# Weight loads that cast on their way, and two-kilobyte q and k loads, in a fused sliding-window attention and MLP kernel

## The chip, the cores and the metric

The kernel runs on one core of one Trainium2 chip. The metric is the device time of one execution in microseconds (us). The profile lists busy time of a tensor engine (PE), VectorE (DVE), ScalarE (ACT) and GpSimd (POOL), and none of SyncE (SP), which issues transfers: 105 in after. ScalarE and GpSimd issue transfers too, between their other instructions (5 and 8 in after). The profile gives the time of the transfers as a share of 16 DMA engines.

## The reference

Attention with a window of 128 tokens and four "sink" tokens that every later token may see, then a two-layer MLP with a quick GELU:

```python
# q, k, v: (4 batches, 8 heads, 768 tokens, 64), float32
scores = (1 / sqrt(64)) * q @ k.T
keep   = (pos_k < 4) | ((0 <= pos_q - pos_k) & (pos_q - pos_k < 128))
a      = softmax(where(keep, scores, -1e9))
x      = (a @ v) as (3072 tokens, 512)
h      = x @ w_in                        # w_in (512, 2048) float32
g      = h / (1 + exp(-1.702 * h))
out    = g @ w_out                       # w_out (2048, 512) float32
```

## The kernel before

The tokens are worked on in 12 blocks of 256. Block k needs its q, k and v (512 KB each in float32), their cast to float16, the transposes of q and k, the scores and the rest of the attention; after it the first layer, which needs `w_in`, and later the second, which needs `w_out`. The two weights are 8 chunks of 1 MB, four of each. Blocks 0 to 2 and the weights have to come in during the first 40 us or so, while the tensor engine is already working on what has arrived.

The order of the instructions on each engine is fixed by a planner that runs when the program is built. It keeps a clock of its own for each engine and one for the transfers, picks the next instruction by priority, and sorts the program by the planned start.

```python
class Plan:
    def run(self, ...):
        dma_free = 0.0                        # ONE clock for all transfers
        ...
            s = max([free[e]] + [after(d, e) for d in o.deps])
            if isinstance(o.engs[e][1], tuple) and len(landed) >= LANES:   # LANES = 8
                s = max(s, landed[-LANES])
        ...
                begin = max(s + 1300, dma_free)       # a transfer begins when those
                dma_free = begin + ns                 # planned before it have ended
                ...
        order.sort(key=lambda x: (x[0], x[1]))        # the program is this ORDER only
```

In the program an instruction waits for data that it reads and for a buffer that it overwrites (one of SyncE's loads of v waited 4.1 us for a cast of v). If it issues a transfer it waits at times for an earlier one that it neither reads nor overwrites: SyncE's loads of q and k waited 1.1 us, in two waits, for v to land. The planner counts this as lanes, eight of them: it issues a transfer when the eighth before it has landed.

The weights are loaded as float32 into a ring of three buffers by SyncE, and cast in halves, 15 of the 16 by GpSimd and one by ScalarE:

```python
    CAST_W = ["POOL ACT"] + ["POOL"] * 7
    def weights(j, at):
        dst = w32[j % RW]                             # RW = 3
        war = reuse("w32", j % RW)
        src = ... 1 MB of moe_w_in (j < 4) or moe_w_out ...
        o_l = op("SP", 400, (2880, 32), lambda: nc.sync.dma_start(dst, src), war, prio=at, kind="w")
        loads.append(o_l)
        for n in range(2):
            to, fr = ...                              # half a chunk
            o = plan.any(cast(1024, CAST_W[j]), lambda e, to=to, fr=fr: copy(e, to, fr), [o_l], ...)

    LOADS = ["a0", "a1", "w0", "w1", "w2", "w3", "a2", "w4", "w5", "w6", "w7"]   # a0: block 0
```

q and k are loaded with two tokens to a partition, which makes runs of 512 bytes in memory; for blocks 0 to 2 (`KT = 3`) they are transposed on the tensor engine, one pair of heads at a time, each pair as soon as its part is there:

```python
        if k == 0:      # three pieces each: q by SyncE, k by ScalarE
            for n, (p0, p1) in enumerate(((0, 1), (1, 2), (2, 4))):
                ...
        else:
            nc.sync.dma_start(dst[:, e], src[b, :, t0 : t0 + TB].rearrange("h (p i) d -> p h i d", i=2))
    ...
        def tp():       # in front(k, p): one pair of heads
            for i in range(2):
                for e in range(2):
                    nc.tensor.transpose(ps[:, e, :, i, :],
                        c16[:, i, e, 2 * p : 2 * p + 2].rearrange("s h d -> s (h d)"), ident)
```

In the first 14 us the tensor engine fills its gaps with matmuls on zeros (line 788 in before), which count as busy (10.2 us in before) and do no work.

The softmax here doesn't subtract the row's maximum and nothing guards it: scores larger than these inputs give would overflow.

## Time and profile before

| | before |
|---|---|
| time, median of 3 | 228.54 us (228.28 to 228.6) |
| span of the profiled execution | 225.9 us |
| tensor engine busy | 216.6 us (96 %) |
| idle time of the tensor engine, 225.9 - 216.6 | 9.3 us |
| tensor engine's share of the chain of waits | 88 % |
| first first-layer matmul | 20.75 us |

From the page of before, the span, the busy times, and two rows of the 40 slices (5.65 us each): the busy share of the DMA engines in tenths and what they moved, in GB/s. Bytes are counted as they are written, which will matter later (in after, the queue with the casting transfers shows 4.19 MB for the 8.39 MB of float32 that they read):

```profile
span 225.9 us, 5365 instructions
PE 216.6 (96%) x2122; PEld 150.2 (66%) x2122; DVE 127.5 (56%) x278; ACT 130.7 (58%) x259; POOL 104.0 (46%) x177
...
DMA  6999999999499999899696895892902402410232
GB/s 169 287 326 375 337 347 352 337 282 239 100 251 288 226 197 220 215 181 288 113 226 176 169 254 121 157 269 61 187 1 49 93 3 46 93 41 8 46 69 70
...
PE 88%; ACT 4%; DVE 3%; DMA 2%; issue 1%; ACTq 0%
```

The last line is the chain of waits. The tensor engine bounds the kernel, so only time in which it is idle or fills gaps can be won. The table by stage of before shows where that is; its columns are the window, its length, busy time (and instructions) of each engine, the granted clock of the tensor engine, the DMA share (the time that packets took, over 16 engines; it comes out above 1 at times and serves here only to tell busy from idle), and GB/s:

```profile
0.00:20.00 20.00, 17.59 (x259) 13.97 (x260) 12.14 (x41) 12.11 (x26) 13.09 (x29) 1.00 0.95 280
20.00:40.00 20.00, 19.39 (x229) 15.59 (x226) 17.10 (x39) 15.07 (x31) 14.89 (x18) 1.00 1.07 347
40.00:60.00 20.00, 20.00 (x159) 13.46 (x157) 8.34 (x17) 7.37 (x13) 17.13 (x27) 1.00 1.06 261
60.00:80.00 20.00, 18.24 (x197) 11.58 (x196) 12.39 (x29) 12.49 (x28) 15.16 (x27) 1.00 1.06 230
```

Apart from the start, the tensor engine loses 0.6 us between 20 and 40 us and 1.8 us between 60 and 80 us, and 4.6 us after 80 us, at the very end. The DMA engines are busy at 90 % and more from 6 to 56 us.

How the weights come in, from the timeline of GpSimd in before (start, length, instruction; in brackets the idle time before it and what ended it):

```profile
18.16 1.04 POOL L274 CAST w_in<-w 128x1024 f16<-128x1024 f32 x1 [0.19 <-DMA w<-in_moe_w_in_dram]
...
20.81 2.03 POOL L274 CAST w_in<-w 128x1024 f16<-128x1024 f32 x2 [1.61 <-DMA w<-in_moe_w_in_dram]
23.57 2.03 POOL L274 CAST w_in<-w 128x1024 f16<-128x1024 f32 x2 [0.73 <-DMA w<-in_moe_w_in_dram]
26.27 2.03 POOL L274 CAST w_in<-w 128x1024 f16<-128x1024 f32 x2 [0.67 <-DMA w<-in_moe_w_in_dram]
```

Each of the last three casts waited for its chunk, so the chunks landed 2.7 us apart. No other load was put among them, as the timeline of SyncE in before shows: the four chunks of `w_in` go out in a row, and block 2's q is issued only after them:

```profile
9.97 10.66 SPq L331 DMA_DIRECT2D w<-in_moe_w_in_dram  x4
20.68 1.35 SPq L385 DMA_DIRECT2D qk<-in_q_dram  x1
...
26.23 3.35 SPq L331 DMA_DIRECT2D w<-in_moe_w_out_dram  x3
```

### The profile page before, as it was taken

What the parts mean: (1) busy time and instruction counts of PE and PEld (TensorE: products, weight loads), DVE (VectorE), ACT (ScalarE), POOL (GpSimd) and SP (SyncE); (2) the same over time, 40 slices, a digit from 0 to 9 for tenths busy, and PEclk for the clock granted to TensorE, in tenths of its full rate; (3) what the DMA queues carried; (4) which work ended last, traced back from release to release, by engine and by line L of the source; (5) the groups of instructions that cost most, each with busy time, mean ns of one, the idle gap of its engine ahead of it and who ended that gap; (6) DMA issues with size and microseconds to landing.
All of it is one profiled execution on the core that took longest, in us unless ns stands there. A gap on an engine that the chain in (4) does not pass through costs nothing.

```text
span 225.9 us, 5365 instructions
## 1 busy us (share of the span) xinstructions
PE 216.6 (96%) x2122; PEld 150.2 (66%) x2122; DVE 127.5 (56%) x278; ACT 130.7 (58%) x259; POOL 104.0 (46%) x177
## 2 busy tenths in 40 slices
PE   8989999999988999999999999999999999999991
PEld 8766886666644776767667667666667667666640
DVE  2677989533376574965565555556457456433400
ACT  3659579154378369746747747645856846445310
POOL 6486777789939981756609729119200000000000
PEclk9999999999999999999999999999999999999999
DMA  6999999999499999899696895892902402410232
GB/s 169 287 326 375 337 347 352 337 282 239 100 251 288 226 197 220 215 181 288 113 226 176 169 254 121 157 269 61 187 1 49 93 3 46 93 41 8 46 69 70
DMA packets 73976, 41.07 MB, mean 182 GB/s; under 512 B 29792, under 2 KB 66784, under 8 KB 73952
## 3 DMA queue, kind: packets, MB, share of 16 engines
q1 hardware_dynamic: 72128, 39.72, 71.2%
q10 hardware_dynamic: 1824, 1.02, 1.6%
q8 instruction: 16, 0.26, 0.5%
q14 instruction: 8, 0.07, 0.1%
HBM read 27.36 MB, written 6.29 MB: 149 GB/s over the span
## 4 chain that ended last, share of the span: by engine, by line
PE 88%; ACT 4%; DVE 3%; DMA 2%; issue 1%; ACTq 0%
PE bank L694 36%; PE bank L722 36%; PE bank L627 6%; PE bank L572 4%; ACT at L590 3%; DMA qk<-in_k_dram 2%; DVE at L597 2%; PE bank L788 2%; PE bank L537 1%; PE bank L511 1%; PE bank L666 1%; ACT ats L545 0%; DVE xn L647 0%; DVE qkT L520 0%; DVE gT L708 0%
## 5 line engine op out<-in xcount | busy, mean ns | idle before, releaser
L722 PE MATMUL bank<-w_out,gT 128*128 128x512 f16 x384 | 99.1, 379 | 0.0
L694 PE MATMUL bank<-xT,w_in 128*128 128x256 f16 x768 | 98.8, 273 | 0.1
L706 ACT ACTIVATE th<-bank 128x512 f16<-128x512 f32 x96 | 57.6, 603 | 62.4 <-PE bank L694 61.5
L708 DVE SCALAR_TENSOR_TENSOR gT<-th,bank 128x512 f16<-128x512 f16 x96 | 65.4, 684 | 49.2 <-ACT th L706 49.1
L694 PEld LDWEIGHTS <-w_in 128*128 128x128 f16 x768 | 73.3, 98 | 21.6 <-issue 2.0
L274 POOL CAST qk<-qk 64x512 f16<-64x512 f32 (+1 forms) x78 | 47.5, 612 | 38.2 <-DMA qk<-in_q_dram 34.4
L590 ACT ACTIVATE at<-bank 128x512 f16<-128x512 f32 (+1 forms) x96 | 50.0, 575 | 5.4 <-PE bank L572 5.0
L722 PEld LDWEIGHTS <-gT 128*128 128x128 f16 x384 | 35.7, 98 | 24.4 <-issue 0.8
L597 DVE TENSOR_TENSOR at<-at,bank 128x1024 f16<-128x1024 f16 (+1 forms) x48 | 30.5, 637 | 20.9 <-ACT at L590 20.8
L274 POOL CAST v<-v 64x512 f16<-64x512 f32 (+1 forms) x48 | 28.6, 595 | 5.0 <-DMA v<-in_v_dram 2.7
L627 PE MATMUL bank<-v,at 128*128 128x65 f16 x352 | 21.4, 193 | 2.0 <-DVE at L597 1.9
L627 PEld LDWEIGHTS <-at 128*128 128x128 f16 x352 | 17.2, 97 | 7.6 <-DVE at L597 3.8
L740 ACT ACTIVATE osb<-bank 128x512 f32<-128x512 f32 (+1 forms) x24 | 14.2, 592 | 11.0 <-PE bank L722 10.9
L545 ACT ACTIVATE ats<-bank 128x256 f16<-128x256 f32 x32 | 12.8, 399 | 9.1 <-PE bank L537 4.5
L647 DVE TENSOR_TENSOR xb<-bank,rcp 128x256 f16<-128x256 f32 x36 | 15.2, 421 | 0.7
L627 PE MATMUL bank<-vs,ats 128*128 128x65 f16 x128 | 15.2, 193 | 0.2 <-DVE gT L708 0.2
L645 DVE RECIPROCAL rcp<-bank 128x4 f32<-128x4 f32 x48 | 8.5, 178 | 10.5 <-PE bank L627 9.9
L627 PEld LDWEIGHTS <-ats 128*128 128x128 f16 x128 | 12.0, 97 | 1.8 <-issue 0.2
L788 PE MATMUL bank<-zero 128*128 128x128 f16 x123 | 10.2, 242 | 1.0 <-DVE zero L287 1.0
L572 PE MATMUL bank<-w 64*128 64x128 f16 (+1 forms) x168 | 10.0, 240 | 0.0
L572 PEld LDWEIGHTS <-w 64*128 64x128 f16 x192 | 6.1, 94 | 5.3 <-issue 5.0
L788 PEld LDWEIGHTS <-zero 128*128 128x128 f16 x123 | 8.7, 111 | 1.5 <-DVE zero L287 1.0
(40 smaller groups left out, 87.0 us busy)
## 6 DMA issues: line engine op xcount, KB each, us to landing
out_dram<-osb SPq DMA_DIRECT2D x47, 128.0 KB, 2.5
qk<-in_q_dram SPq DMA_DIRECT2D x11, 512.0 KB, 5.2
qk<-in_k_dram SPq DMA_DIRECT2D x11, 512.0 KB, 7.2
v<-in_v_dram SPq DMA_DIRECT2D x11, 512.0 KB, 7.9
w<-in_moe_w_in_dram SPq DMA_DIRECT2D x4, 1024.0 KB, 8.5
w<-in_moe_w_out_dram SPq DMA_DIRECT2D x4, 1024.0 KB, 9.2
qk<-in_q_dram SPq DMA_DIRECT2D x2, 128.0 KB, 3.0
qk<-in_k_dram ACTq DMA_DIRECT2D x2, 128.0 KB, 4.2
```

The costliest lines, as they stand in the source:

```text
L274: {"POOL": nc.gpsimd.tensor_copy, "DVE": nc.vector.tensor_copy, "ACT": nc.scalar.copy}[e](out=out, in_=in_)
L572: nc.tensor.matmul(f32(o_s, 2 * n + i)[:, c : c + w], src[d, j], Q[d].rearrange("d j s -> d (j s)")[:, q0 : q0 + w], start=True, stop=True,)
L590: nc.scalar.activation(out=A[:, i, 0:W], in_=f32(o_s, 2 * n + i)[:, 0:W], func=AF.Exp, scale=scale)
L597: nc.vector.tensor_tensor(out=A[:, :, 0:W], in0=A[:, :, 0:W], in1=mask[:, c0 : c0 + W].unsqueeze(1).to_broadcast((P, 2, W)), op=ALU.mult,)
L627: nc.tensor.matmul(avp()[:, j, i], a_, v_, start=(n == 0), stop=(n == len(mms) - 1))
L647: o_n = op("DVE", 300, 425, lambda: nc.vector.tensor_tensor(out=X, in0=avp()[:, :, :, 0:D], in1=rc.to_broadcast((P, 2, 2, D)), op=ALU.mult ...
L694: nc.tensor.matmul(f32(holder[0])[:, bass.ts(e, TB)], w_in16[:, c, bass.ts(Fi, P)], X[:, c] if k < KX else X2[:, :, c], start=(c == 0), st ...
L706: o_t = op("ACT", 477, 600, lambda first=first: nc.scalar.activation(out=th[first.places[0]], in_=f32(first), func=AF.Tanh, scale=0.851), ...
L708: o_g[k, s] = op("DVE", 565, 690, lambda first=first, s=s: nc.vector.scalar_tensor_tensor(out=g[:, 2 * s : 2 * s + 2].rearrange("p a t -> ...
L722: nc.tensor.matmul(f32(holder[0]), g[:, Fi, bass.ts(j, P)], w_out16[:, Fi], start=(Fi == 0), stop=(Fi == NF - 1),)
L740: nc.scalar.mul(O[:, c], f32(holder[0])[:, c], 0.5)
L788: nc.tensor.matmul(warm_bank[:, 0:P], zero, zero, start=True, stop=True)
```

## The change

The intent seems to be to spare GpSimd the casts of the weights (15 of 1.04 us), which stand in front of casts that the attention needs, and to move q and k of the first blocks in longer runs.

1. q and k of blocks 0 to 2 are loaded with eight tokens to a partition, in runs of 2 KB, half of the heads at a time. The transposes go through a permutation matrix in place of the identity, which puts the rows back in order, and now need both halves.
2. Each chunk of weights is loaded by one transfer that casts to float16 on its way. GpSimd issues it.
3. In the plan, the first loads are held back until the transfers ahead of them are down to a given length ("gated by transfer time"), lanes are counted for each queue, and two constants change.

```diff
-RING, LANES, SLACK = 163, 8, 2500
+RING, LANES, SLACK = 163, 8, 700
@@ in the planner
-            if isinstance(o.engs[e][1], tuple) and len(landed) >= LANES:
-                s = max(s, landed[-LANES])
+            line = landed[e == "POOL"]
+            if isinstance(o.engs[e][1], tuple) and len(line) >= LANES:
+                s = max(s, line[-LANES])
@@
-    KT, KX, AHEAD = 3, 3, globals().get('OPT',{}).get('AHEAD',2)
+    KT, KX, AHEAD = 3, 3, globals().get('OPT',{}).get('AHEAD',0)
@@ weights
-        o_l = op("SP", 400, (2880, 32), lambda: nc.sync.dma_start(dst, src), war, prio=at, kind="w")
-        loads.append(o_l)
-        for n in range(2):
-            ...
-            o = plan.any(cast(1024, CAST_W[j]), lambda e, to=to, fr=fr: copy(e, to, fr), [o_l], prio=at, kind="cw")
+        o_w[j] = op("POOL", 780, (2800, 33), lambda: nc.gpsimd.dma_start(to, src), prio=at, kind="w")
+        loads.append(o_w[j])
@@ planned order of the loads
-    LOADS = [... "w2", "w3", "a2", "w4", "w5", "w6", "w7"]
+    LOADS = [... "w2", "w3", "w4", "a2", "w5", "w6", "w7"]
@@ q and k of blocks 0 to 2
-                    nc.sync.dma_start(dst[:, e], src[b, :, t0 : t0 + TB].rearrange("h (p i) d -> p h i d", i=2))
+                for h in range(2):
+                        dma.dma_start(
+                            dst[:, e].rearrange("p h i d -> p (h i d)")[:, 512 * h : 512 * h + 512],
+                            src[b, h::2, t0 : t0 + TB].rearrange("p (g i) d -> g p (i d)", i=8),
+                        )
@@ transposes of blocks 0 to 2
-                        ps[:, e, :, i, :], c16[:, i, e, 2 * p : 2 * p + 2].rearrange("s h d -> s (h d)"), ident
+                nc.tensor.transpose(f16(o_tp)[:, bass.ts(a, P)], C[:, a].rearrange("s h d -> s (h d)"), perm)
@@ the gate, at the end
+    for n, o in enumerate(loads):
+        if 8 <= n < 4 + 5 * KT + 8:
+            m, ahead = n - 1, 0.0
+            while ahead < (3200 if o.kind == "w" else 2600):
+                ahead += next(iter(loads[m].engs.values()))[1][0]
+                m -= 1
+            o.deps.append(loads[m])
```

(Cut: the casts into the new layout, the copies out of PSUM, a later planned start of GpSimd's transfers, the memory that the float32 weight ring gives back, and code moved between functions.)

More of the change, by code (lines that the diff above doesn't have):

```diff
@@ L80, in run @@
         dma_free = 0.0
-        ring, landed = {e: [] for e in ENGINES}, []
+        ring, landed = {e: [] for e in ENGINES}, {True: [], False: []}
         order = []
@@ L161, in run @@
                 free[e] = t
-                begin = max(s + 1300, dma_free)
+                begin = max(s + (2000 if e == "POOL" else 1300), dma_free)
                 dma_free = begin + ns
                 ring[e].append((begin, dma_free, nd))
-                landed.append(dma_free + 900)
+                landed[e == "POOL"].append(dma_free + 900)
                 o.end = dma_free + 900 + (SLACK if o.kind in ("turn", "xturn") else 0)
@@ L214 @@
     PAIRED_FROM, RR = 2, 3
-    KT, KX, AHEAD = 3, 3, globals().get('OPT',{}).get('AHEAD',2)
+    KT, KX, AHEAD = 3, 3, globals().get('OPT',{}).get('AHEAD',0)
     RB = 4
-    RS, RQ, RV, RKT, RA, RX, RG, RTH, RO, RW = 3, 2, 4, 9, 6, 3, 5, 3, 3, 3
+    RS, RQ, RV, RA, RX, RG, RTH, RO = 3, 2, 4, 6, 3, 5, 3, 3
     pool = ctx.enter_context(tc.tile_pool(name="sb", bufs=1))
@@ L229 @@
     seen = pool.tile([P, 2 * P], FP16, name="seen")
+    perm = pool.tile([P, P], FP16, name="perm")
     dummy = pool.tile([P, 8], FP16, name="dummy")
@@ L233 @@
     w_out16 = pool.tile([P, NF, d_model], FP16, name="w_out16")
-    w32 = ring("w32", RW, (P, 4, 512), FP32)
-    blkT = [t.rearrange("p c f -> p (c f)")[:, 1024 * n : 1024 * n + 1024].bitcast(FP16)
-            .rearrange("d (e p j s) -> d e p j s", e=2, p=NP, j=2) for t in w32 for n in range(2)][:RB]
+    blkT = ring("blkT", RB, (P, 2, NP, 2, P), FP16)
     vs16 = pool.tile([P, B, NP, 2, E], FP16, name="vs16")
@@ L243 @@
     v16 = ring("v16", RV, (P, 2, H, E), FP16)
-    qkT = ring("qkT", RKT, (P, 2, 2, P), FP16)
     at = ring("at", RA, (P, 2, 512), FP16)
@@ L309 @@
     o_mask = op("PE", 7 * pe_ns(P), 7 * pe_ns(P) + 200, masks, [o_seen], prio=NEVER + 3, kind="const")
+    o_perm = op("DVE", 130, 230, lambda: nc.vector.tensor_copy(
+        out=perm.rearrange("r (h g) -> r h g", h=NP), in_=ident.rearrange("r (g h) -> r h g", h=NP)),
+        [o_ident], prio=NEVER + 2.8, kind="const")
     o_vs0 = op("POOL", 2200, 2300, lambda: nc.gpsimd.memset(vs16, 0.0), prio=NEVER + 3, kind="const")
@@ L315 @@
     OPT = globals().get("OPT", {})
-    CAST_W = ["POOL ACT"] + ["POOL"] * 7
     CAST_QK = ["DVE ACT", "POOL ACT"] + ["POOL"] * (NK - 2)
     CAST_V = ["POOL ACT", "POOL"] + ["POOL"] * (NK - 2)
-    CAST_W, CAST_QK, CAST_V = OPT.get("W", CAST_W), OPT.get("QK", CAST_QK), OPT.get("V", CAST_V)
-    o_win, o_wout = {}, {}
+    CAST_QK, CAST_V = OPT.get("QK", CAST_QK), OPT.get("V", CAST_V)
+    o_w = {}
     loads = []
     def weights(j, at):
-        dst = w32[j % RW]
-        war = reuse("w32", j % RW)
         if j < 4:
             src = moe_w_in[:, bass.ts(j, 512)].rearrange("(c p) f -> p c f", p=P)
+            to = w_in16[:, :, bass.ts(j, 512)]
         else:
             src = moe_w_out[bass.ts(j - 4, 512), :].rearrange("(c p) f -> p c f", p=P)
-        o_l = op("SP", 400, (2880, 32), lambda: nc.sync.dma_start(dst, src), war, prio=at, kind="w")
-        loads.append(o_l)
-        for n in range(2):
-            if j < 4:
-                c = slice(512 * j + 256 * n, 512 * j + 256 * n + 256)
-                to, fr = w_in16[:, :, c], dst[:, :, bass.ts(n, 256)]
-            else:
-                to, fr = w_out16[:, 4 * (j - 4) + 2 * n : 4 * (j - 4) + 2 * n + 2], dst[:, 2 * n : 2 * n + 2]
-            o = plan.any(cast(1024, CAST_W[j]), lambda e, to=to, fr=fr: copy(e, to, fr), [o_l], prio=at, kind="cw")
-            uses("w32", j % RW, o)
-            (o_win if j < 4 else o_wout)[2 * (j % 4) + n] = o
+            to = w_out16[:, 4 * (j - 4) : 4 * (j - 4) + 4]
+        o_w[j] = op("POOL", 780, (2800, 33), lambda: nc.gpsimd.dma_start(to, src), prio=at, kind="w")
+        loads.append(o_w[j])
     L = OPT.get('L',17300.0)
-    LOADS = OPT.get("LOADS") or ["a0", "a1", "w0", "w1", "w2", "w3", "a2", "w4", "w5", "w6", "w7"]
+    LOADS = OPT.get("LOADS") or ["a0", "a1", "w0", "w1", "w2", "w3", "w4", "a2", "w5", "w6", "w7"]
     def load_at(x):
@@ L358, in slots, with eights @@
         return c16.rearrange("s i e h d -> s (i e h d)").rearrange("s (e p j x) -> s e p j x", e=2, p=NP, j=2)
+    def eights(c16):
+        return c16.rearrange("s i e h d -> s (i e h d)").rearrange("s (e i a h d) -> s e i a h d", e=2, i=2, a=4, h=2)
     o_cqk, o_cv, o_vs = {}, {}, {}
@@ L370, in load, with f @@
         lq = {}
-        if k == 0:
-            for n, (p0, p1) in enumerate(((0, 1), (1, 2), (2, 4))):
-                for e, (eng, dma, src) in enumerate((("SP", nc.sync, q), ("ACT", nc.scalar, k_ap))):
-                    def f(p0=p0, p1=p1, e=e, dma=dma, src=src):
+        for e, src in enumerate((q, k_ap)):
+            eng, dma = ("ACT", nc.scalar) if k == 0 and e else ("SP", nc.sync)
+            lq[e] = []
+            if k < KT:
+                for h in range(2):
+                    def f(e=e, h=h, src=src, dma=dma):
                         dma.dma_start(
-                            dst[:, e, 2 * p0 : 2 * p1],
-                            src[b, 2 * p0 : 2 * p1, t0 : t0 + TB].rearrange("h (p i) d -> p h i d", i=2),
-                        )
-                    o = op(eng, 500, (600 * (p1 - p0), 16 * (p1 - p0)), f, war, prio=NEVER + 2.5 + n / 8, kind="load")
-                    for p in range(p0, p1):
-                        lq[p, e] = o
-        else:
-            for e, src in enumerate((q, k_ap)):
-                def f(e=e, src=src):
-                    nc.sync.dma_start(
-                        dst[:, e], src[b, :, t0 : t0 + TB].rearrange("h (p i) d -> p h i d", i=2)
-                    )
-                o = op("SP", 450, (1720, 64), f, war, prio=prio + e / 2, kind="load")
-                loads.append(o)
-                for p in range(NP):
-                    lq[p, e] = o
+                            dst[:, e].rearrange("p h i d -> p (h i d)")[:, 512 * h : 512 * h + 512],
+                            src[b, h::2, t0 : t0 + TB].rearrange("p (g i) d -> g p (i d)", i=8),
+                        )
+                    lq[e].append(op(eng, 450, (700, 8), f, war, prio=prio + (h / 2 + e / 8 if k == 0 else e / 2 + h / 8), kind="load"))
+            else:
+                def f(e=e, src=src, dma=dma):
+                    dma.dma_start(dst[:, e], src[b, :, t0 : t0 + TB].rearrange("h (p i) d -> p h i d", i=2))
+                lq[e].append(op(eng, 450, (1720, 64), f, war, prio=prio + e / 2, kind="load"))
+            loads.extend(lq[e])
         def lv(dma, h):
@@ L395, in load @@
         if k == 0:
-            o_lv = [op("SP", 500, (900, 32), lv(nc.sync, slice(0, 4)), war, prio=NEVER + 2.7, kind="load"),
-                    op("ACT", 500, (900, 32), lv(nc.scalar, slice(4, 8)), war, prio=NEVER + 2.95, kind="load")]
+            o_lv = [op(e, 500, (900, 32), lv(dma, slice(4 * n, 4 * n + 4)), war, prio=prio + 0.7 + n / 8, kind="load")
+                    for n, (e, dma) in enumerate((("SP", nc.sync), ("ACT", nc.scalar)))]
             loads.extend(o_lv)
@@ L404, in load @@
         war = reuse("qk16", k % RQ)
-        w = 2 if k == 0 else 4
         if k >= KT:
@@ L413, in f @@
                                  dst[64 * j : 64 * j + 64, e, :, i].rearrange("s (p h) d -> s p h d", h=2))
-                        o = plan.any(cast(512, CAST_QK[k]), f, [lq[0, e]] + war, prio=nominal(k - 1, -7), kind="cqk")
+                        o = plan.any(cast(512, CAST_QK[k]), f, lq[e] + war, prio=nominal(k - 1, -7), kind="cqk")
                         o_cqk[k, 2 * e + j, i] = o
-        for h0 in range(0, H if k < KT else 0, w):
-            for e in range(2):
-                def f(eng, h=slice(h0, h0 + w), e=e):
-                    copy(eng, c16[:, :, e, h].rearrange("s i h d -> s h i d"), dst[:, e, h])
-                ps = range(h0 // 2, (h0 + w) // 2)
-                o = plan.any(cast(P * w, CAST_QK[k]), f, [lq[p, e] for p in ps] + war,
-                             prio=nominal(k - 1, -7 + h0) if k else NEVER + h0, kind="cqk")
-                for p in ps:
-                    o_cqk[k, p, e] = o
+        else:
+            C = eights(c16)
+            for h in range(2):
+                for e in range(2):
+                    def f(eng, e=e, h=h):
+                        copy(eng, C[:, e, :, :, h].rearrange("s i a d -> s a i d"),
+                             dst[:, e].rearrange("s h i d -> s (h i d)").rearrange("s (h a i d) -> s h a i d", h=2, a=4, i=2)[:, h])
+                    o_cqk[k, e, h] = plan.any(cast(512, CAST_QK[k]), f, [lq[e][h]] + war,
+                                              prio=nominal(k - 1, -7 + 2 * h) if k else NEVER + h, kind="cqk")
         for o in {id(x): x for (kk, _, _), x in o_cqk.items() if kk == k}.values():
@@ L460, in turned @@
     def turned(k, p, e):
-        return blkT[k % RB][:, e, p] if k >= KT else qkT[(NP * k + p) % RKT][:, e]
+        return blkT[k % RB][:, e, p]
     def hold(k, p, o):
-        uses(*(("blkT", k % RB) if k >= KT else ("qkT", (NP * k + p) % RKT)), o)
+        uses("blkT", k % RB, o)
     def turn(k):
@@ L471, in turn @@
         c16, T = qk16[k % RQ], blkT[k % RB]
-        war = reuse("blkT", k % RB) + ([o for x in range(RW) for o in reuse("w32", x)] if k == KT else [])
-        casts = [o_cqk[k, p, e] for p in range(NP) for e in range(2)]
-        def f():
-            nc.sync.dma_start_transpose(
-                T.rearrange("d e p j s -> d (e p j) s"), slots(c16).rearrange("s e p j x -> s (e p j x)")
-            )
-        o_t = [op("SP", 1600, (3600, 128), f, casts + war, prio=base - 9 * h8, kind="turn")]
-        uses("qk16", k % RQ, o_t[0])
+        war = reuse("blkT", k % RB)
+        o_t = []
+        if k < KT:
+            for i in range(2):
+                for e in range(2):
+                    o_t.append(turn_on_pe(k, e, i, T, eights(c16)[:, e, i], war))
+        else:
+            o_t.append(turn_by_dma(k, T, slots(c16), war))
         for p in range(NP):
@@ L495, in turn, with turn_on_pe, tp, turn_by_dma @@
                 o_ks[b, p] = o
+    def turn_on_pe(k, e, i, T, C, war):
+        base = attend(k, 0) - 5 * L / 8
+        def tp():
+            for a in range(4):
+                nc.tensor.transpose(f16(o_tp)[:, bass.ts(a, P)], C[:, a].rearrange("s h d -> s (h d)"), perm)
+        o_tp = op("PE", 4 * pe_ns(P), 3 * pe_ns(P) + P / 2.4 + 166, tp, [o_cqk[k, e, 0], o_cqk[k, e, 1], o_perm],
+                  prio=base + 2 * i + e, acq=("t", 1), kind="tp")
+        uses("qk16", k % RQ, o_tp)
+        return plan.any({"DVE": (590, 700), "ACT": (487, 600)}, lambda eng: copy(
+            eng, T[:, e].rearrange("d p j s -> d (p j) s")[:, :, 64 * i : 64 * i + 64].rearrange("d n (g a) -> d n g a", a=4),
+            f16(o_tp).rearrange("d (a n g) -> d n g a", a=4, g=16)),
+            [o_tp] + war, prio=base + 2 * i + e, rel=[(o_tp, 0)], kind="cp")
+    def turn_by_dma(k, T, C, war):
+        casts = [o_cqk[k, p, e] for p in range(NP) for e in range(2)]
+        def f():
+            nc.sync.dma_start_transpose(
+                T.rearrange("d e p j s -> d (e p j) s"), C.rearrange("s e p j x -> s (e p j x)")
+            )
+        o = op("SP", 1600, (3600, 128), f, casts + war, prio=attend(k, 0) - 9 * L / 8, kind="turn")
+        uses("qk16", k % RQ, o)
+        return o
     def front(k, p):
@@ L502, in front @@
         h8 = L / 8
-        c16 = qk16[k % RQ]
-        T = qkT[u % RKT]
         Q = turned(k, p, 0)
-        def tp():
-            ps = f16(o_tp).rearrange("d (e j i p) -> d e j i p", e=2, j=2, i=2)
-            for i in range(2):
-                for e in range(2):
-                    nc.tensor.transpose(
-                        ps[:, e, :, i, :], c16[:, i, e, 2 * p : 2 * p + 2].rearrange("s h d -> s (h d)"), ident
-                    )
-        if k < KT:
-            war = reuse("qkT", u % RKT)
-            o_tp = op("PE", 4 * pe_ns(P), 3 * pe_ns(P) + P / 2.4 + 166, tp,
-                      [o_cqk[k, p, 0], o_cqk[k, p, 1], o_ident] + war, prio=base - 5 * h8, acq=("t", 1), kind="tp")
-            uses("qk16", k % RQ, o_tp)
-            o_cp = op("DVE", 331, 430, lambda: nc.vector.tensor_copy(
-                out=T, in_=f16(o_tp).rearrange("d (e j s) -> d e j s", e=2, j=2)),
-                [o_tp] + war, prio=base - 5 * h8, rel=[(o_tp, 0)], kind="cp")
-            o_qkT[k, p] = [o_cp]
-        As = ats[u % RA]
-        if r == 0 and k < KT:
-            def ks():
-                for i in range(2):
-                    d = slice(64 * i, 64 * i + 64)
-                    nc.gpsimd.tensor_copy(
-                        out=ks16[d, NP * b + p].rearrange("d (i a) -> d i a", i=2)[:, :, 32 * i : 32 * i + 2],
-                        in_=T[d, 1, 0].rearrange("d (i a) -> d i a", i=2)[:, :, 0:2],
-                    )
-            o_ks[b, p] = op("POOL", 260, 400, ks, [o_cp, o_ks0], prio=base - 4 * h8, kind="ks")
-            uses("qkT", u % RKT, o_ks[b, p])
+        As = ats[u % RA]
         if r:
@@ L697, in f @@
                         )
-                deps = [o_xT[k, p] for p in range(NP)] + [o_win[Fi // 2]] + ([last] if last else war_g)
+                deps = [o_xT[k, p] for p in range(NP)] + [o_w[Fi // 4]] + ([last] if last else war_g)
                 o = op("PE", 4 * pe_ns(TB), 3 * pe_ns(TB) + TB / 2.4 + 166, f, deps, prio=prio + e,
@@ L725, in f @@
                         )
-                deps = [o_g[k, s], o_wout[s]] + ([prev] if prev else [])
+                deps = [o_g[k, s], o_w[4 + s // 2]] + ([prev] if prev else [])
                 o = op("PE", 2 * pe_ns(512), pe_ns(512) + 512 / 2.4 + 166, f, deps,
@@ L763 @@
         load(k_)
-        if k_ >= KT:
-            turn(k_)
+        turn(k_)
         for p_ in range(NP):
```

## The prediction

> **What bounds the kernel now.** The tensor engine: 96% busy on the page (216.6 of 225.9 us), 88% of the chain of waits, at full clock. The instruction order of both kernels shows the same needed matmuls (768 first-layer, 384 second-layer, 480 value, 256 score, 48 q/k transposes); only dummy warm-up matmuls go from 123 to 114. With the timeline's issue spacings (109 ns for 128x256, 217 ns for 128x512, 56 ns for 128x128) needed work is about 206 us (my estimate). So some 20 us are lost, and only those can be won:
> - Start, about 13.5 us: by 23.6 us some 10 us of needed work is done; the first first-layer matmul starts at 20.75.
> - 33 to 40 us, about 1.5 us: block 2's exponentials and masks.
> - 56 to 79 us, 1.7 us idle (stage table): attention of blocks 3 and 4 comes late.
> - Tail, 4.6 us: untouched.
>
> **What the change does.**
> 1. q, k of blocks 0-2 (3 MB) move in 2 KB runs. The stage table shows 250 to 310 GB/s where 512 B runs dominate, 370 to 390 where weights (2 KB runs) do: about 2.5 us less transfer by block 2. [...]
> 2. Block 0's transposes now need whole q and k, so its first scores slip from 6.5 to about 8.3 us, but all head pairs are then ready together (before, pairs 2 and 3 at 12 us). Block 0's attention should end near 14.5 instead of 17.3 us.
> 3. 16 weight casts go (1.02 us each on GpSimd): about 15 us of GpSimd, plus three fp32 buffers and their reuse waits. The first weight chunk was usable near 20 us; I expect 16. GpSimd pays 8 issues. [...] I assume 2.7 to 3.2 us per chunk.
> 4. PSUM copies of q, k grow from 0.42 to about 0.6 us (x12), partly on ScalarE.
> 5. Block 3's casts no longer queue behind weight casts (GpSimd ended those at 45.1 us), so its attention comes earlier.
>
> **On the critical path.** The first layer starts near 16 us, with about 5 us of needed work done instead of 7. ScalarE and VectorE then limit (each over 10 us of work between 16 and 27 us), so only about 2.5 us of start loss goes. The loss at 33 to 40 hardly changes; of that at 56 to 79 about 1 us goes. Sum 3.6 us. From 80 us on only the position of attention changes (AHEAD 2 to 0), worth nothing on a saturated engine.
>
> **Prediction: 224.9 us, range 222.3 to 227.7.** Faster by over 2% (below 224.0): 0.36; within 2%: 0.61; slower by over 2%: 0.03.
>
> **What would show it.** Right: first-layer matmuls from 15 to 17.5 us; block 2's scores at 34 to 36 us; GpSimd busy near 90 us; idle at 55 to 80 us below 1 us; tail unchanged. Step 2 is wrong if first scores come after 9.5 us; step 3 if weight chunks land over 3.5 us apart.
>
> **What would make it wrong.** Casting transfers much slower than plain ones, so that second-layer matmuls wait for w_out at 30 to 40 us; GpSimd held at a gated issue while casts behind it are needed; the smaller allowance after DMA transposes (2500 to 700) placing scores too early, with tensor waits in blocks 3 to 11; or ScalarE and VectorE coping better than I think, which gives 5 us or more.

(The sum came to 3.6 us: about 2.5 us at the start, hardly anything at 33 to 40 us, about 1 us at 56 to 79 us. The 2.7 to 3.2 us for a casting chunk were an assumption: no run had shown the speed of a casting transfer, and the one at hand was that of a plain chunk, 2.73 us in before.)

## More of the kernel before

A dependency that was only in the plan leaves no wait behind.

A stretch that holds almost nothing but weights gives the speed of a plain transfer. From the DMA view of before between 34 and 38 us:

```profile
DMA packets 773, 1.54 MB, mean 386 GB/s; under 512 B 19, under 2 KB 19, under 8 KB 773
```

A chunk is 512 rows of 2 KB. The page of after counts 4,224 packets on the queue that carries the eight chunks alone, 528 for each: one for a row, and 16 more. (They are small ones: where three chunks moved alone, e1 between 18 and 26 us, 46 of 1,594 packets were under 512 bytes.) So a chunk takes 528 / 773 x 4 us = 2.73 us, as the casts have it.

The plan is an order of instructions for each engine, nothing more.

## The result, and the profile after

| | before | after |
|---|---|---|
| time, median of 4 of the same rounds | 228.57 us (228.28 to 228.69) | 231.76 us (231.46 to 232.27) |
| span of the profiled execution | 225.9 us | 229.7 us |
| tensor engine busy | 216.6 us | 215.8 us |
| idle time of the tensor engine | 9.3 us | 13.9 us |
| GpSimd busy | 104.0 us | 93.0 us |
| first scores of block 0 | 6.54 us | 11.36 us |
| first first-layer matmul | 20.75 us | 21.50 us |

The ratio is 1.0144, with a 95 % interval of 1.012 to 1.0168: 1.4 % slower. A ratio is the mean time of one kernel's runs over that of the other's in the same rounds, so it isn't quite the ratio of the medians quoted.

The page of after, the same lines:

```profile
span 229.7 us, 5319 instructions
PE 215.8 (94%) x2113; PEld 150.1 (65%) x2113; DVE 128.4 (56%) x271; ACT 133.3 (58%) x263; POOL 93.0 (40%) x163
...
DMA  6999999978099999879599587688732222230232
GB/s 188 332 329 231 216 216 217 220 202 167 21 214 272 272 202 190 209 145 245 144 187 293 103 198 204 125 159 221 146 41 46 57 37 49 59 75 6 46 84 53
...
PE 82%; DMA 10%; POOL 4%; issue 1%; SPq 1%; ACT 0%; DVE 0%; POOLq 0%
```

The tensor engine does the same work. DMA has gone from 2 % of the chain to 10 %. The low GB/s from the fourth slice on isn't slowness by itself: a casting transfer reads 2 KB for each 1 KB that it writes and counts half (1,423 packets of weights are 1.42 MB below, though each is a row of 2 KB read). The pages of both kernels have 27.36 MB of HBM read.

The table by stage of after:

```profile
0.00:20.00 20.00, 15.91 (x215) 13.37 (x215) 10.82 (x31) 10.88 (x24) 12.92 (x25) 1.00 0.98 277
20.00:40.00 20.00, 15.46 (x179) 12.34 (x178) 13.30 (x28) 11.34 (x23) 12.96 (x21) 1.00 1.20 217
40.00:60.00 20.00, 20.00 (x200) 13.73 (x199) 12.28 (x26) 11.76 (x24) 11.73 (x22) 1.00 0.82 172
60.00:80.00 20.00, 19.86 (x208) 13.47 (x206) 13.08 (x30) 14.83 (x31) 8.68 (x15) 1.00 0.93 217
```

Against before, the tensor engine is busy 1.7 us less in the first stage (part of that is fill), 3.9 us less in the second, the same in the third and 1.6 us more in the fourth: together 4.0 us less, and the span is 3.8 us longer. (After 80 us its idle time is 5.1 us, in before 4.6 us.) So the loss lies before 40 us, and above all between 20 and 40 us. What the tensor engine waited for there is in its waits in after (total us, times, longest); before had no line of this kind, no wait for a transfer at all:

```profile
PE bank L675 <- DMA w_in<-in_moe_w_in_dram: 3.8, 4, 1.4
...
PE bank L703 <- DMA w_out<-in_moe_w_out_dram: 0.7, 1, 0.7
```

And when, from the timeline of the tensor engine in after (line 553: scores; 675: first layer; 703: second layer):

```profile
11.36 0.50 PE L553 MATMUL bank<-blkT 64*128 64x256 f16 x8 [0.87 <-ACT blkT L272]
...
21.50 1.05 PE L675 MATMUL bank<-xT,w_in 128*128 128x256 f16 x8 [1.36 <-DMA w_in<-in_moe_w_in_dram]
...
25.05 0.61 PE L675 MATMUL bank<-xT,w_in 128*128 128x256 f16 x4 [0.35 <-DMA w_in<-in_moe_w_in_dram]
...
28.89 0.61 PE L675 MATMUL bank<-xT,w_in 128*128 128x256 f16 x4 [0.80 <-DMA w_in<-in_moe_w_in_dram]
...
32.60 1.05 PE L675 MATMUL bank<-xT,w_in 128*128 128x256 f16 x8 [1.30 <-DMA w_in<-in_moe_w_in_dram]
...
36.22 1.02 PE L703 MATMUL bank<-w_out,gT 128*128 128x512 f16 x4 [0.72 <-DMA w_out<-in_moe_w_out_dram]
```

Five chunks in turn are waited for, 3.6 to 3.8 us apart, where before had 2.7. What else moved in that time? The DMA view of after between 24 and 34 us, by queue (q0 is GpSimd's, q1 SyncE's; packets, MB written, share of the 16 engines):

```profile
q0 software_dynamic: 1423, 1.42, 83.6%
q1 hardware_dynamic: 1415, 0.71, 35.2%
```

A packet of weights is a row of 2 KB read, one of SyncE's a row of q, k or v of 512 bytes, and the two queues moved them in nearly equal numbers, 1,423 and 1,415. (The traces count packets; in what order the engines took them isn't shown.) 528 / 1423 x 10 us gives 3.71 us for a chunk, as the waits have it.

Who issued those rows shows in the timelines of SyncE (SPq) and GpSimd (POOL) in after:

```profile
8.53 2.00 SPq L370 DMA_DIRECT2D qk<-in_q_dram  x2
...
13.28 0.53 SPq L377 DMA_DIRECT2D qk<-in_q_dram  x1
14.01 4.11 SPq L377 DMA_DIRECT2D qk<-in_k_dram  x1
```

```profile
10.11 1.77 POOL L272 CAST v<-v 64x256 f16<-64x256 f32 x4 [5.80 <-DMA v<-in_v_dram]
...
12.33 0.88 POOL L331 DMA_DIRECT2D w_in<-in_moe_w_in_dram  x1
```

Line 370 at 8.53 us is q of block 2, line 377 is block 3. SyncE issued block 2 before GpSimd had issued its first chunk of weights, because that issue stood behind casts of v which waited 5.8 us for v. In the given order of loads five chunks come ahead of block 2 (`a2`); in the run the first of them was issued 3.8 us after block 2's q, and block 3's first load went out one microsecond after it. The list of SyncE's waits in after names earlier transfers of its own and engines that free its buffers; none names a transfer of `w_in` or `w_out`. The gate is in the plan, as an order; in the program, nothing holds SyncE's queue back for GpSimd's.

### The profile page after: what moved, and what is told of

Its sections match the earlier page's. It is cut to its first block, busy times and chain, and to the rows that moved or that the text cites. A ratio compares the mean times of both kernels' runs of the same rounds, so it can differ in the third digit from the quotient of the medians. Undisturbed runs are those within 1.5% of the kernel's fastest.

```text
span 229.7 us, 5319 instructions
## 1 busy us (share of the span) xinstructions
PE 215.8 (94%) x2113; PEld 150.1 (65%) x2113; DVE 128.4 (56%) x271; ACT 133.3 (58%) x263; POOL 93.0 (40%) x163
## 3 DMA queue, kind: packets, MB, share of 16 engines
q1 hardware_dynamic: 64112, 31.33, 60.2%
q0 software_dynamic: 4224, 4.19, 10.8%
q10 hardware_dynamic: 1040, 1.02, 1.5%
HBM read 27.36 MB, written 6.29 MB: 147 GB/s over the span
## 4 chain that ended last, share of the span: by engine, by line
PE 82%; DMA 10%; POOL 4%; issue 1%; SPq 1%; ACT 0%; DVE 0%; POOLq 0%
PE bank L703 36%; PE bank L675 34%; DMA w_out<-in_moe_w_out_dram 7%; PE bank L608 5%; PE bank L553 4%; DMA v<-in_v_dram 3%; POOL v L272 2%; PE bank L518 1%; POOL vs L435 1%; POOL w_in L331 1%; SPq L370 1%; ACT osb L721 0%; PE bank L486 0%; POOL qk L272 0%; PE bank L647 0%
## 5 line engine op out<-in xcount | busy, mean ns | idle before, releaser
L675 PE MATMUL bank<-xT,w_in 128*128 128x256 f16 x768 | 101.4, 273 | 3.8 <-DMA w_in<-in_moe_w_in_dram 3.8
L675 PEld LDWEIGHTS <-w_in 128*128 128x128 f16 x768 | 72.2, 98 | 27.3 <-DMA w_in<-in_moe_w_in_dram 4.9
L272 POOL CAST qk<-qk 64x512 f16<-64x512 f32 (+1 forms) x77 | 47.0, 611 | 55.0 <-DMA qk<-in_q_dram 44.1
L571 ACT ACTIVATE at<-bank 128x512 f16<-128x512 f32 (+1 forms) x96 | 49.5, 570 | 11.8 <-PE bank L553 11.8
L553 PE MATMUL bank<-blkT 64*128 64x256 f16 x192 | 13.1, 243 | 1.0 <-ACT blkT L272 0.9
L553 PEld LDWEIGHTS <-blkT 64*128 64x128 f16 x256 | 8.2, 94 | 7.8 <-issue 6.1
```

Source lines behind the costliest of these rows:

```text
L272: {"POOL": nc.gpsimd.tensor_copy, "DVE": nc.vector.tensor_copy, "ACT": nc.scalar.copy}[e](out=out, in_=in_)
L553: nc.tensor.matmul(f32(o_s, 2 * n + i)[:, c : c + w], src[d, j], Q[d].rearrange("d j s -> d (j s)")[:, q0 : q0 + w], start=True, stop=True,)
L571: nc.scalar.activation(out=A[:, i, 0:W], in_=f32(o_s, 2 * n + i)[:, 0:W], func=AF.Exp, scale=scale)
L675: nc.tensor.matmul(f32(holder[0])[:, bass.ts(e, TB)], w_in16[:, c, bass.ts(Fi, P)], X[:, c] if k < KX else X2[:, :, c], start=(c == 0), st ...
```

## The experiments

Three theories stood at the start. A: the transfers of the two queues share the DMA engines, and loads of later blocks run ahead of the weights. B: a transfer that casts is slow in itself. C: the reworked q and k loads and transposes cost the time. A fourth, D, was that the changed constants place the attention badly. "Before" was measured, with medians of 228.28 to 228.69 us.

| run | what | median us | ratio to before (95 %) |
|---|---|---|---|
| e1_gate | after, real waits before blocks 2 and 3 | 229.88 | 1.0048 (0.9978 to 1.0119) |
| e2_weights_only | before, with the casting weights alone | 237.01 | 1.0389 (1.0319 to 1.0459) |
| e3_loads_only | after, with the old weights | 227.08 | 0.9942 (0.9881 to 1.0002) |
| e4_old_constants | after, with the old constants | 231.57 | 1.0143 (1.0086 to 1.02) |
| e5_gate_early | after, earlier gate, block 2 last | 231.77 | 1.0125 (1.0066 to 1.0184) |
| e6_one_queue | after, blocks 2 and 3 on GpSimd's queue | 232.23 | 1.013 (1.006 to 1.02) |
| e7_v_casts_later | after, v of block 0 cast later | 231.0 | 1.0087 (1.0031 to 1.0144) |
| e8_ordered | e10, weights issued earlier, v cast later | 228.55 | 0.9986 (0.9934 to 1.0038) |
| e9_plain_second_queue | e3, its plain weights on GpSimd's queue | 236.07 | 1.0319 (1.0274 to 1.0364) |
| e10_one_queue_gated | e6, one wait before block 4 | 226.09 | 0.9887 (0.9834 to 0.9939) |
| e11_v_casts_later_gated | e10 with e7 | 225.3 | 0.9856 (0.979 to 0.9922) |
| e12_k_on_sync | e11, block 0's k on SyncE's queue | 224.66 | 0.9827 (0.975 to 0.9904) |

### e1_gate: a real wait

A transfer of 16 bytes that reads a chunk of weights is issued by SyncE ahead of a block's loads. Since it reads what GpSimd's transfer writes, the program makes SyncE wait for that chunk. In the trace SyncE issued the 16-byte transfer at 27.94 us, about when the fourth chunk landed, some 8.6 us after its issue at 19.28 us, and block 2's q at 28.81 us.

```diff
+    GATE = {2: 3, 3: 6}      # block 2 waits for w3 (last of w_in), block 3 for w6
+            loads.append(op("SP", 60, (50, 1), lambda: nc.sync.dma_start(gated[...], fr), [o_w[j]], ...))
```

> The changed kernel with two real waits added: a 16-byte transfer that reads the fourth w_in chunk stands on SyncE's queue before the loads of block 2, one that reads the third w_out chunk before those of block 3, so SyncE's later loads cannot run ahead of the weights. Theory A (sharing): SyncE's loads of blocks 2 and 3 overtake the weights[...]; then with the waits the chunks land 2.7 to 3.0 us apart instead of 3.7, the fifth lands near 30 us instead of 36.2, the tensor engine's idle time for weights falls from 4.5 us to under 1.5 us, and the time falls to 227 to 229 us. Theory B (casting itself is slow): chunks stay 3.6 us or more apart also when nothing else moves, and the time stays at 231 us or grows. Theory C (the reworked q/k loads and transposes cost the time): no change in time beyond 0.5 us.

Measured: 229.88 us, so 1.9 us less than after, though a little above what A expected. The waits for `w_in` are gone. The DMA view between 18 and 26 us, with weights alone on the engines:

```profile
q0 software_dynamic: 1593, 1.58, 121.7%
```

528 / 1593 x 8 us = 2.65 us for a chunk with its cast (1 MB read, so about 396 GB/s by this estimate), against 2.73 us for a plain one in before, at 386 GB/s. That ends B: the cast costs nothing that can be measured. The rest of the gain was lost at a new place. From the timeline of GpSimd in this run:

```profile
32.31 0.61 POOL L273 CAST qk<-qk 128x512 f16<-128x512 f32 x1 [11.54 <-DMA qk<-in_q_dram]
32.86 0.74 POOL L332 DMA_DIRECT2D w_out<-in_moe_w_out_dram  x1
```

The second chunk of `w_out` stood in GpSimd's order behind a cast of block 2, which the gate now held back for 11.5 us; the DMA engines were all but idle at 28 to 30 us (share 0.13, 21 GB/s), and the tensor engine waited 1.7 us for `w_out`.

### e2_weights_only and e3_loads_only: one half at a time

e2 is before with only the weights changed to casting transfers of GpSimd (and with the planner's lanes for each queue and later start of GpSimd's transfers, which go with them). e3 is after with the weights back on SyncE's queue as plain transfers, with the casts, and in the old planned order of loads. One of its four `blkT` buffers lies in a weight buffer, as all did in before.

```diff
e2, to before:
-        o_l = op("SP", 400, (2880, 32), lambda: nc.sync.dma_start(dst, src), war, ...)   (and 2 casts)
+        o_w[j] = op("POOL", 780, (2800, 33), lambda: nc.gpsimd.dma_start(to, src), prio=at, kind="w")
e3, to after:
-        o_w[j] = op("POOL", 780, (2800, 33), lambda: nc.gpsimd.dma_start(to, src), prio=at, kind="w")
+        o_l = op("SP", 400, (2880, 32), lambda: nc.sync.dma_start(dst, src), war, ...)   (and 2 casts)
```

> The kernel before with only the weights changed: casting transfers from GpSimd's queue, no fp32 staging and no weight casts; q and k loads, transposes and plan constants as before. Theory A: the loads of blocks 2 and 3 on SyncE's queue run beside the weights and both share the engines, chunks 3.5 us or more apart in the shared stretch; 230 to 233 us, slower than before. Theory B: the same, but with chunks slow also where SyncE's queue is empty. Theory C: no loss against before, 227 to 228.5 us.

> The changed kernel with only the weights put back: plain transfers of fp32 chunks on SyncE's one queue and casts on GpSimd; q and k in runs of eight tokens, transposes through the permutation and the new plan constants stay. Theories A and B: the loss is gone, and the faster loads gain a little against before: 226 to 228.5 us, chunks 2.7 us apart. Theory C: the loss stays, 230 to 232 us, with first scores near 11 us and the first layer starting later than before's 20.75 us.

Measured: e2 237.01 us, worse than any theory had it; e3 227.08 us, a little faster than before (its interval just reaches 1). So the new loads and transposes are no cost, and C falls; all the loss comes with the weights. In e2 the sharing shows from the other side. Its packets between 26 and 34 us are 1,147 of weights and 1,149 of SyncE's, again one to one, and the longest wait of its tensor engine, at 32 to 37 us, is for a cast of block 2's k, which had itself waited 5.9 us for k to land:

```profile
PE bank L502 <- POOL qk L275: 4.8, 1, 4.8
```

There it was the weights, all issued by 18.5 us, that held up a block. So in these two runs one of the two was late, and not the same one. Not all of e2's loss need be sharing: behind that wait the granted clock of its profiled execution was one half for some 6.8 us (35 to 42 us; the page shows 5 tenths there, and eight first-layer matmuls took 1.91 us at 37.74 us in place of 1.04 us at 29.77 us), which by estimate is worth up to 3.4 us (half of it) of the tensor engine, and no run separates the two.

### e4_old_constants

```diff
-RING, LANES, SLACK = 163, 8, 700
+RING, LANES, SLACK = 163, 8, 2500
-    ... AHEAD',0)
+    ... AHEAD',2)
```

> The changed kernel with the two plan constants as before (allowance after a DMA transpose 2500, AHEAD 2): only the order of instructions from block 3 on differs. All of theories A, B and C put the loss before 45 us, so the time stays within 1 us of 231.8. If it falls by 2 us or more, a fourth theory holds: the new order of the later blocks costs the time.

Measured: 231.57 us, ratio 1.0143 against after's 1.0144. D falls.

### e5_gate_early: let the blocks in sooner

e1 lost time because the gate opened late. Here block 2 waits for the third chunk only, the `w_out` chunks are issued right behind `w_in`, and block 3 has no gate.

```diff
-    LOADS = [..., "w3", "w4", "a2", "w5", "w6", "w7"]
+    LOADS = [..., "w3", "w4", "w5", "w6", "w7", "a2"]
+    GATE = {2: 2}
```

> The run with real waits left the DMA engines idle for 2 us, because block 2 waited for the fourth chunk while GpSimd held the later chunks back behind block 2's casts. Here block 2's loads wait for the third w_in chunk instead, GpSimd issues all w_out chunks right behind the fifth, block 2 is planned behind all weights, and block 3 has no wait of its own (it follows block 2 on SyncE's queue). Theory A: no stretch of 2 us with a DMA share under 0.5 before 35 us, no wait of the tensor engine for w_in; 226 to 228.5 us, below the first run with waits (229.9). If the time stays at 229.5 or more, something else than the order of transfers costs it.

Measured: 231.77 us; the expectation failed. The first stage went as meant and no `w_in` was waited for, but SyncE's loads were issued from 24.8 us, their rows moved from 28 us on, and the sharing was back, now with `w_out`:

```profile
PE bank L710 <- DMA w_out<-in_moe_w_out_dram: 4.8, 4, 2.3
```

The four chunks of `w_out` were waited for at 32.04, 36.23, 39.95 and 43.99 us, some 4 us apart. Between 34 and 40 us the packets are one to one again (853 and 852). The slow chunks move with the time at which SyncE's loads run beside them. That is A again, in another place.

### e6_one_queue: the same loads on the same queue

If the order across queues is the fault, the loads of blocks 2 and 3 can go on GpSimd's queue among the weights.

```diff
-            eng, dma = ("ACT", nc.scalar) if k == 0 and e else ("SP", nc.sync)
+            eng, dma = ("ACT", nc.scalar) if k == 0 and e else ("POOL", nc.gpsimd) if k in (2, 3) else ("SP", nc.sync)
(and v of these blocks likewise)
```

> The changed kernel with the loads of blocks 2 and 3 issued from GpSimd too, in the planned order, so that one queue holds weights and loads and no added wait is needed. Theory A: w_in chunks 2.6 to 2.9 us apart as in the run with waits, no tensor wait for w_in over 0.5 us, 227 to 230 us (GpSimd pays eight more issues of about 0.75 us or more each). Theory B, which the run with waits already speaks against (1593 packets of 2 KB in 8 us, 2.6 us a chunk, when casting transfers moved alone), would keep 231 us or more.

Measured: 232.23 us; the expectation failed. The loads of block 4 were still SyncE's, and with nothing ahead of them they were issued at 15.7, 16.9 and 19.8 us, ahead of blocks 2 and 3 and of most weights. Between 24 and 32 us:

```profile
q0 software_dynamic: 1139, 1.13, 83.5%
q1 hardware_dynamic: 1137, 0.57, 35.4%
```

### e10_one_queue_gated: one wait more

e6, with a 16-byte transfer that reads the last chunk of `w_out` ahead of block 4's loads.

```diff
+        if k == 4:
+            loads.append(op("SP", 60, (50, 1), lambda: nc.sync.dma_start(gated[0:1, 0:8], w_out16[0:1, 12, 0:8]),
+                            [o_w[7]], prio=prio - 0.1, kind="gate"))
```

> The one-queue run showed that block 4's loads, left on SyncE's queue, ran ahead in their turn (issued from 15.7 us; chunks 3.7 us apart from 23 us on). Here one wait is added: block 4's loads stand behind a 16-byte transfer that reads the last w_out chunk. Theory A: with nothing on SyncE's queue the w_in chunks come 2.5 to 2.8 us apart, w_in waits of the tensor engine under 0.3 us, first-layer matmuls of block 0 done by 29.5 us instead of 32.6, and the time falls by 2 to 4 us against the one-queue run (232.2), to 228 to 230 us.

Measured: 226.09 us, 6.1 us less than e6 (ratio 0.9887 against 1.013, which is 5.6 us; the two were measured in different calls), better than expected, and below before. Block 4's loads now went out at 43 us. The tensor engine has no wait for a transfer left, and is busy 19.89 us between 20 and 40 us. Between 19 and 25 us GpSimd's queue is alone:

```profile
q0 software_dynamic: 1154, 1.14, 120.1%
```

That is 528 / 1154 x 6 us = 2.75 us for a chunk. The order of instructions in the two programs is the same on every engine but for this one transfer of SyncE and its wait, which makes it the cleanest test of A. Not all of the 6 us is its work, though: in the profiled executions e10 was 0.7 us ahead before the wait could matter (first scores at 10.62 us against 11.35 us).

### e9_plain_second_queue: the second queue without a cast

e3, whose plain weights SyncE issues, with one edit: GpSimd issues them. Nothing is cast on the way.

```diff
-        o_l = op("SP", 400, (2880, 32), lambda: nc.sync.dma_start(dst, src), war, prio=at, kind="w")
+        o_l = op("POOL", 780, (2880, 32), lambda: nc.gpsimd.dma_start(dst, src), war, prio=at, kind="w")
```

> The run with only the loads changed (weights plain on SyncE's queue, 227.1 us) with one difference: the plain weight transfers are issued from GpSimd's queue, with no cast in the transfer and the same casts on GpSimd afterwards. It puts the same plain weights on a second queue. Theory A: SyncE's loads of blocks 2 and 3 run ahead, the two queues alternate packet for packet (counts within 5% of each other between 24 and 32 us), chunks come 3.5 us or more apart, and the time rises by 3 us or more, to 230 to 234 us. If the cast in the transfer were what costs: it stays at 227 to 228.5 us.

(That the queues alternate was inferred from counts such as 1,423 and 1,415 in after.)

Measured: 236.07 us, 9 us more than e3. The timeline of GpSimd shows the chunks of `w_in` landing as in after, not as in before:

```profile
23.84 2.02 POOL L275 CAST w_in<-w 128x1024 f16<-128x1024 f32 x2 [0.90 <-DMA w<-in_moe_w_in_dram]
27.57 2.03 POOL L275 CAST w_in<-w 128x1024 f16<-128x1024 f32 x2 [1.71 <-DMA w<-in_moe_w_in_dram]
31.35 2.03 POOL L275 CAST w_in<-w 128x1024 f16<-128x1024 f32 x2 [1.75 <-DMA w<-in_moe_w_in_dram]
```

They are 3.7 and 3.8 us apart, with no cast in the transfer: the second queue does it. The packets between 16 and 24 us:

```profile
q0 software_dynamic: 633, 2.46, 82.9%
q1 hardware_dynamic: 626, 0.51, 20.1%
```

They are one to one there, although a packet of this plain queue held 3.9 KB, two rows, and one of SyncE's 0.8 KB on average. Other stretches of this run are not: 319 to 829 between 15 and 20 us, 302 to 590 between 24 and 28 us. In the stretch for which the count was expected, 24 to 32 us, it failed: 449 to 1,930, and why isn't shown. The 9 us aren't all sharing. GpSimd has the weights' casts again and issues them too, so that a chunk is issued only when the casts ahead of it are done (at 33.3 us the first of `w_out`, when the casts that began at 31.35 us ended, and at 46.9 us the last). And the granted clock of the profiled execution was one half for some 6.8 us (21 to 28 us; 0.83 on average between 20 and 40 us); by estimate that is worth up to 3.4 us (half of 6.8), though the four times (235.99 to 236.17 us) don't follow their mean clocks (0.982 to 0.992). How the 9 us split stays open. The intervals of the chunks, which are transfers, are what e9 shows.

### e7_v_casts_later and e11: the late start

In after, ScalarE made one copy of block 0's transposes out of PSUM at 8.15 us and its next only at 10.73 us, because casts of v stood between them in its order and waited for v until 10.0 us. These casts can come after.

```diff
+        if k_ == 0:
+            for o_ in {id(x): x for p_ in range(NP) for x in o_cv[0, p_]}.values():
+                o_.deps += o_qkT[0, 0]
```

> The changed kernel with only block 0's v casts moved behind the four PSUM copies of block 0 in the order of ScalarE and VectorE. In the changed kernel ScalarE waited until 10.0 us for v before its second copy, and block 0's first scores came at 11.36 us. Expected: first scores at 9.8 to 10.4 us. As the first layer waits for its first weight chunk (21.4 us), the time should stay within 0.7 us of the changed kernel's (231.8). If it falls by 1.5 us or more, block 0's attention was on the critical path after all.

> The one-queue run with block 4's loads behind the last chunk (226.1 us), and block 0's v casts moved behind the PSUM copies as in the v-cast run (first scores there at 9.89 us, 0.8 us of time). The first layer there began at 19.3 us and waits for the first weight chunk, whose issue still stands behind the v casts on GpSimd (11.6 us). Expected: first scores near 9.9 us, 225.3 to 226.5 us; it tells whether block 0's lateness costs anything once the weights' order is mended.

Measured: with the edit on after (e7), first scores at 9.89 us, as expected, in place of 11.36, and 231.0 us in place of 231.76. Of these 1.47 us some 0.6 aren't the edit's: k's second half was cast at 7.91 us in place of 8.54. (The granted clock of its profiled execution was one half from 18 to 24 us, 0.56 between 20 and 25 us; I don't know why, and read nothing from its later stages.) With the edit on e10 (e11), 225.3 us against 226.09; first scores at 10.39 us, later than the 9.9 expected, because the second half of k was cast only at 8.19 us.

### e8_ordered: a miss

e10, with v cast later and the first two chunks of weights issued ahead of v's casts; in the plan the gate no longer holds for loads that GpSimd issues.

```diff
+            o_early = op("POOL", 80, 180, ...)       # waits for block 0's q and k
+            for j_ in (0, 1):
+                o_w[j_].deps.append(o_early)
+                o_.behind = o_w[1]                   # v's casts come after weights 0 and 1
```

> The version that the runs point to, with casting transfers kept: one queue for weights and the loads of blocks 2 and 3, block 4's loads behind the last chunk, and GpSimd issues the first two weight chunks ahead of block 0's v casts (about 10 us instead of 12.3), with those v casts behind the PSUM copies. Expected from theory A: first weight chunk at 17 to 18 us, first layer from about 17.5 us, 225 to 228 us. If over 229 us, GpSimd's in-order queue (weights' issues, lanes, casts) still holds something back.

Measured: 228.55 us, worse than e10. The weights were issued at 11.15 us, but v's casts began on GpSimd only at 12.85 us in place of 9.38 us in e10, block 0's attention ended later, and the first layer came at 21.09 us in place of 19.27 us in e10. (The granted clock of its profiled execution was 0.92 over the first 20 us; the four times, 228.29 to 229.24 us, agree all the same.) What was put first on GpSimd made the rest late.

### e12_k_on_sync: the order of block 0's own loads

e11, with block 0's k issued by SyncE, so that one queue has q, k, q, k in this order; until then ScalarE's k had been in flight beside SyncE's q, v and block 1.

```diff
-            eng, dma = ("ACT", nc.scalar) if k == 0 and e else ("POOL", nc.gpsimd) if k in (2, 3) else ("SP", nc.sync)
+            eng, dma = ("POOL", nc.gpsimd) if k in (2, 3) else ("SP", nc.sync)
```

> The same, and block 0's k halves issued from SyncE's queue in the order q, k, q, k, ahead of v and of block 1, instead of from ScalarE's. In the changed kernel the second half of k was cast only at 8.54 us though ScalarE issued it by 2.5 us, because SyncE's v and block 1 loads ran beside it. Theory A for the start: all of q and k land by 6.5 to 7 us, the last q/k cast of block 0 starts by 7.2 us, first scores at 8.3 to 9.2 us. Time 224.8 to 226.3 us. If the second half of k still comes after 8 us, the sharing of queues was not what delayed it.

Measured: 224.66 us (224.37 to 224.96), the fastest of all, ratio 0.9827 to before. The last piece of k, from VectorE's timeline:

```profile
7.13 0.43 DVE L273 CAST qk<-qk 128x512 f16<-128x512 f32 x1 [0.17 <-DMA qk<-in_k_dram]
```

In after this was at 8.54 us. The second half of k had been issued by ScalarE by 2.5 us there and took 6.6 us to land; beside it SyncE's v and block 1 moved (565 packets of SyncE's and 516 of ScalarE's between 6 and 8.5 us). The first scores came at 9.80 us, so the expected 8.3 to 9.2 was missed. The first layer started at 18.86 us and the tensor engine was busy without a gap from 20 to 60 us.

## Why the prediction was wrong, point by point

The sum was 3.6 us of gain; the kernel lost 3.2 us.

**Where it failed: step 3.** "The first weight chunk was usable near 20 us; I expect 16. ... I assume 2.7 to 3.2 us per chunk." The chunks were waited for at 21.50 us and then every 3.6 to 3.8 us, past the 3.5 us that the prediction itself set as the mark of step 3 being wrong. It named a slow cast as what could go wrong; that was not it: alone on the engines a casting chunk takes 2.65 us (e1) or 2.75 us (e10), a plain one 2.73 us. The assumption that failed is the one that was not written down: that transfers land in the planned order, as the weights and the blocks after the first had in before (chunks 2.7 us apart), while SyncE issued them all. The prediction took "gated" for a wait, while the gate lives only in the plan. With the weights on GpSimd's queue, SyncE's loads of blocks 2 and 3 were free to run ahead; as many of their rows moved as rows of weights, and chunks went from 2.73 to 3.71 us. Between 20 and 40 us the tensor engine was busy 3.9 us less than in before; with the order held it is busy 19.89 us there (e10), more than before's 19.39. (That the first chunk was usable at 21.50 us and not at 16 has a second cause, its late issue; see what stays open.) A wait that holds the other queue back, in a program otherwise the same, moves the time by 5.6 to 6.1 us (e6 to e10); a plain transfer on the second queue shows the same intervals (e9); the old weights on SyncE's queue take the loss away (e3).

The prediction asked what the cast would cost and not what else would be in flight. The trace of after shows what was: 1,423 packets of weights and 1,415 of SyncE's in the same 10 us.

**Step 2 failed as well, at a smaller price.** First scores were expected at 8.3 us and came at 11.36 us; block 0's attention, expected to end near 14.5, ended at about 20 us, where before took until about 17. Two causes, both of order: k's second half landed late, beside loads needed later (e12 brings its cast from 8.54 to 7.13 us), and v's casts stood ahead of a PSUM copy (e7 brings the scores to 9.89 us). Even with both mended the scores were at 9.80 us, so 8.3 was too early in any case; and the first layer was at 18.86 us in the best version, not 16. The copies of step 4 are as predicted in size (0.57 to 0.69 us) but stand in a chain of casts, transposes and copies which the prediction summed too short.

**What was right.** The needed matmuls are the same (the tensor engine is busy 216.6 and 215.8 us). The 2 KB runs help rather than hurt: the loads by themselves are at worst even (e3). GpSimd is busy 93.0 us, "near 90". Between 60 and 80 us, 1.6 of the 1.8 us lost in before were won, where step 5 expected about 1 us. Its reason, the weights' casts gone from GpSimd, isn't shown: in e3 these casts are back, and the tensor engine is busy 19.82 us there all the same. From 80 us on little changed. The constants are worth nothing (e4). Block 2's scores, predicted at 34 to 36 us, came at 43.40 us; with the order held they come at 38.84 us (e10) and 36.93 us (e12), so most of that delay goes with step 3.

**The size of what was to be gained** was near enough. With the transfers in the order that the prediction took for granted, the change runs in 224.66 us, beside a prediction of 224.9. It gets there by another path than the one predicted (a later first layer, with no gap after it) and with k moved as well, so this agreement is no proof of the sum.

**What stays open.** GpSimd's first issue at 12.33 us delays the weights too, and no run changes that alone: e8 tried and delayed v instead, and e12 brought it to 9.71 us along with other things. The steps from e10 to e11 and e12 are 0.8 and 0.6 us; the runs of e11 and e12 don't overlap, those of e10 and e11 overlap, so the step from e10 to e11 is not secured.

## What to carry to other kernels

When loads move from one issuing engine to another, ask of every transfer in flight on the other queues what now keeps it from running ahead; an order in a plan or a priority is no wait. Here two busy queues moved nearly equal numbers of packets (1,423 and 1,415 in after, 1,147 and 1,149 in e2, 1,139 and 1,137 in e6; with a plain transfer on the second queue not always: 302 and 590 in e9), so that rows of 512 bytes, needed later and a fifth of the bytes read, stretched the chunks needed now from 2.73 to 3.71 us. Where order matters, put the transfers on one queue (k's last cast at 7.13 us in e12, at 8.54 us in after), and hold the other queue by a wait on data, such as a tiny transfer that reads what must land first (232.23 to 226.09 us here). And look at what stands in front of an issue on an engine that also computes: here an issue took 0.74 to 0.88 us of GpSimd, the first chunk was issued at 12.33 us, behind casts that had waited 5.8 us, and one of `w_out` in e1 at 32.86 us, behind a cast that had waited 11.5 us.
